# Attention's instructions in source order on every engine, the branch on one partition, masks built inside the branch

## The chip, the cores and the metric

One core of a Trainium2 chip runs the kernel. The metric is the device time of one execution in microseconds. Before the change the median of 3 runs was 667.44 us (664.49 to 668.09).

## What is computed

A windowed attention with sink keys, and two feed-forward layers behind it, in float32.

```python
scores = scale * np.matmul(q, k.transpose(0, 1, 3, 2))     # q, k, v: 2 x 8 heads x 768 x 64
keep = (pos[None, :] < n_sink) | ((rel >= 0) & (rel < window))   # n_sink 4, window 128
a = softmax(np.where(keep, scores, -1e9))
x = np.matmul(a, v)                                         # -> 1536 tokens x 512
h = x @ w_in                                                # 512 x 2048
g = np.where(h > 0, h, np.exp(np.minimum(h, 0)) - 1)
x = g @ w_out                                               # 2048 x 512
h = x @ w2_in
out = (np.maximum(h, 0) + alpha * np.minimum(h, 0)) @ w2_out
```

The weights come as float64, two 32-bit words each, and `n_sink` and `window` as 64-bit integers.

## The kernel before, in words

The program first loads the two limits (`ints`, L186), the first keys, queries, values and weights, works out from the limits whether the fast path may be taken (`flag_i`, L223), builds masks 0 and 1 (`make_mask_at`, L457) and branches (L721) into `fast_path` or `general_path`. Only the fast path runs here.

Queries are cut into blocks of 110 (seven per head), keys into the 128 to 256 columns that a block can see. Two heads lie in one 128-partition tile. A unit (`units`, L139) is one or two blocks of two heads; there are 32 units. Each unit goes through `scores` (TensorE score matmuls `qk`, L489; VectorE adds the mask and takes the extreme, L496; ScalarE takes the exponential with its sum, L501), `normalised` (two small VectorE operations, L511 and L514; GpSimd scales, L518), `transposed` (TensorE transposes `t`, L532; VectorE copies them to `pt`, L608) and `values` (TensorE value matmuls `x`, L553; ScalarE makes `xh`, L562, and VectorE the rest `xl`, L563). `matmul3` makes one product out of three with numbers split into a high and a low part (`xh`, `xl`, `wh`, `wl`, `gh`, `gl`).

The loop over steps s (L581) does, for each s, the scores of unit s, the values of unit s-2, one piece of fill, the normalisation of unit s and the transposes of unit s-1. Fill is round 0 of the first feed-forward layer for tokens whose attention is done: 32 pieces `g1` (`h`, L278 in `matmul3`) and `g2` (`o`) of 12 matmuls each over 220, 328 or 440 tokens. A step without fill gets a group of dummy matmuls (`keep_busy`, L238). `after` of a `g1` piece is ScalarE's L307 and L308, VectorE's `u` (L309), ScalarE's `gh` (L320) and GpSimd's `gl` (L321). In the first eight steps one half of round 0's weights is decoded in each (`decode_w`): two ScalarE instructions (L254, L255), four VectorE ones (L257, L260, L263, L266), ScalarE's `wh` (L269), and `wl` (L270) on VectorE for halves 0 to 3 and on GpSimd for 4 to 7. The raw weights have three buffers, the tiles `wx` and `wr` that a decode works in two.

Behind the loop `mlp_rounds` does the last token tile of round 0 and seven more rounds over three tiles of 512 tokens, each with eight more decodes for the round that follows.

A planner sets the order of the instructions on each engine's queue. It goes by the order of the source as priority, and by its own estimate of when an instruction can start: whatever can start goes first, so instructions of later code (of `mlp_rounds`, too) move ahead into gaps. Tiles are given out by the same planner.

Of the kernel before, what the change touches and what calls it, by code (L numbers as in the profile page):

```python
# [13 lines left out]
I32 = mybir.dt.int32  # L14
# [40 lines left out]
MS = {2: 1, 3: 2, 4: 5}  # L55
# [56 lines left out]
def attention_mlp2(  # L112
# [86 lines left out]
    for g in range(HP):  # L199
        if g:  # L200
            load_kq(g)
        if g < WPRE:
            o = HP * (2 * KTOT[0] + VCH[0] * 2 * D) + g * 2 * DM
            load_w(0, g, 0, room[:, o : o + 2 * DM].bitcast(I32).rearrange("p (n t) -> p n t", t=2))
        load_v(g)
    wfirst = dict(wraw)
    intf = const.tile([P, 2, 2], F32, tag="intf", name="intf")
# [9 lines left out]
    flag_f = const.tile([P, 2], F32, tag="flag_f", name="flag_f")  # L217
    flag_i = const.tile([P, 1], I32, tag="flag_i", name="flag_i")
    nc.vector.tensor_scalar(out=flag_f[:, 0:1], in0=win, scalar1=float(WIN), scalar2=None, op0=ALU.is_le)
    nc.vector.scalar_tensor_tensor(  # L220
        out=flag_f[:, 1:2], in0=win, scalar=1.0, in1=flag_f[:, 0:1], op0=ALU.is_ge, op1=ALU.mult
    )
    nc.vector.scalar_tensor_tensor(  # L223
        out=flag_i, in0=ns, scalar=float(SINK), in1=flag_f[:, 1:2], op0=ALU.is_le, op1=ALU.mult
    )
# [19 lines left out]
    def decode_w(pool, m, fc, io, sub=None):  # L245
# [35 lines left out]
    class Mlp:  # L281
# [7 lines left out]
        def g1(self, m, c0, n, fc):  # L289
# [12 lines left out]
            def after():  # L302
# [9 lines left out]
                else:  # L312
# [6 lines left out]
                    )  # L319
                nc.scalar.copy(gh, u)  # L320
# [5 lines left out]
        def g2(self, m, c0, n, r, d):  # L326
# [11 lines left out]
            def after():  # L338
# [4 lines left out]
                if r == NR - 1:  # L343
                    if m == 0:
                        xh, xl = (x[:, d, c0 : c0 + n] for x in xs)
                        nc.scalar.copy(xh, a)
                        nc.gpsimd.tensor_tensor(out=xl, in0=a, in1=xh, op=ALU.subtract)
                    else:
                        nc.sync.dma_start(out=out_t[d * P : d * P + P, c0 : c0 + n], in_=a)

            return after

    def run(pieces):

        pend = []
        for p, extra in pieces:
            if p is None:
                pend.pop(0)()
# [4 lines left out]
            if len(pend) > 1:  # L363
                pend.pop(0)()
        for a in pend:
            a()
# [6 lines left out]
    def mlp_rounds(mlp, items, wpools):  # L373
# [22 lines left out]
        def weights_step():  # L396
# [3 lines left out]
            for _ in decode_w(*order[j]):  # L400
                pass
# [25 lines left out]
    def make_mask(blk, rel, mk):  # L427

        for c, n, k in mask_runs(blk):
            k = 4 * S if k is None else k  # L430
            nc.gpsimd.iota(rel[:, c : c + n], pattern=[[-1, n]], base=Q0[blk] - k, channel_multiplier=1)
        nc.vector.tensor_scalar(
            out=mk, in0=rel.bitcast(U32), scalar1=win, scalar2=-NEG / SCALE, op0=ALU.is_ge, op1=ALU.mult
# [5 lines left out]
        masks[blk] = mk  # L439
# [12 lines left out]
    def make_mask_at(blk):  # L452
        o = sum(KW[i] for i in MASKS if i < blk)
        rel = tmp.tile([P, WMAX], I32, tag="rel", name=f"rel{blk}", bufs=1)
        make_mask(blk, rel[:, : KW[blk]], mask_t[:, o : o + KW[blk]])

    make_mask_at(0)  # L457
    make_mask_at(1)
# [4 lines left out]
    def fast_path():  # L463
# [10 lines left out]
        def scores(i):  # L474
# [6 lines left out]
            for blk in blks:  # L481
                n, (k0, w) = NQ[blk], SPAN[blk]
                for e in range(2):
# [7 lines left out]
                    )  # L491
            for j, blk in enumerate(blks):
# [12 lines left out]
            soft[i] = sb, st  # L505
# [33 lines left out]
        def values(i):  # L539
# [21 lines left out]
            def after():  # L561
                nc.scalar.copy(xh, px[:, :o])  # L562
# [215 lines left out]
```

## Time and profile before

| | before |
|---|---|
| median of 3 runs | 667.44 us |
| profiled execution | 667.86 us |
| its span, first to last instruction | 666.0 us |
| TensorE busy | 637.4 us, 96% |
| VectorE busy | 440.4 us, 66% |
| ScalarE busy | 313.9 us, 47% |
| GpSimd busy | 210.2 us, 32% |
| mean granted TensorE clock | 0.977 |

Busy time of TensorE is modelled, so a share of 96% does not say that it runs at its peak. In the rows PE is TensorE, PEld its weight loads, DVE VectorE, ACT ScalarE, POOL GpSimd, SP SyncE; L278 is line 278 of the kernel; PEclk is the granted clock as a share of 2.4 GHz, at full or at half. `out<-in` names the tiles.

### The profile page before, as it was taken

To read this page: it belongs to the slowest core of one execution; us is meant where nothing else is said; L and a number is where in the kernel's file an instruction comes from. 1 tells how busy PE (TensorE), PEld (TensorE's weight loads), DVE (VectorE), ACT (ScalarE), POOL (GpSimd) and SP (SyncE) were. 2 spreads that over 40 slices of the span, in tenths; PEclk is the share of its full clock that TensorE was granted. 3 is DMA by queue.
4 is the path that set the end of the run, shared out by engine and by line. 5 is a ranking of instruction groups with operands and counts; after the bars stand their busy time and mean duration, and the time that the engine had idled before them with its cause. 6 is when DMAs were issued, how large, how long until landed. Compare 5 with 4: busy or idle time off the path is not lost.

```text
span 666.0 us, 9595 instructions
## 1 busy us (share of the span) xinstructions
PE 637.4 (96%) x3412; PEld 524.9 (79%) x3412; DVE 440.4 (66%) x932; ACT 313.9 (47%) x710; POOL 210.2 (32%) x253
## 2 busy tenths in 40 slices
PE   6977999999989898999999999999999999999996
PEld 5646888888878676888888888888888888888885
DVE  5798566756399998576656786785569673443332
ACT  5576576747378775466546743543525220110010
POOL 3455344534122322232215364332123212331130
PEclk8796999999999999999999999999999999999999
DMA  7766325630034243031103120311212000000112
GB/s 225 209 169 186 105 66 134 156 101 2 1 126 158 95 135 118 2 126 63 64 21 107 63 64 5 122 64 63 65 63 64 32 0 1 0 2 0 64 50 83
DMA packets 21657, 52.87 MB, mean 79 GB/s; under 512 B 2656, under 2 KB 9824, under 8 KB 21600
## 3 DMA queue, kind: packets, MB, share of 16 engines
q1 hardware_dynamic: 21168, 52.05, 25.6%
q8 instruction: 29, 0.48, 0.3%
q14 instruction: 28, 0.23, 0.1%
q10 hardware_dynamic: 432, 0.12, 0.1%
HBM read 49.01 MB, written 3.15 MB: 78 GB/s over the span
## 4 chain that ended last, share of the span: by engine, by line
PE 78%; DVE 13%; ACT 3%; issue 2%; DMA 2%; POOL 1%; SPq 0%; ACTq 0%; DVEq 0%; POOLq 0%
PE o L278 36%; PE h L278 33%; PE x L553 4%; PE qk L489 3%; PE t L532 3%; DVE wx L263 3%; DVE wx L266 2%; DVE wx L257 2%; DVE wl L270 2%; DVE wx L260 1%; ACT s L501 1%; DVE pt L608 1%; DVE u L309 1%; DMA acc<-in_w_dram 1%; PE busy L238 1%
## 5 line engine op out<-in xcount | busy, mean ns | idle before, releaser
L321 POOL TENSOR_TENSOR gl<-u,gh 128x512 fp32r<-128x512 f32 (+3 forms) x104 | 131.9, 1268 | 339.0 <-ACT gh L320 330.5
L278 PE MATMUL o<-gh,wh 128*128 128x512 f32 (+3 forms) x416 | 157.4, 379 | 5.7 <-DVE u L309 5.7
L278 PE MATMUL h<-xh,wh 128*128 128x512 f32 (+3 forms) x416 | 158.2, 380 | 0.0
L278 PE MATMUL o<-gl,wh 128*128 128x512 f32 (+3 forms) x416 | 155.9, 375 | 1.0 <-POOL gl L321 0.9
L278 PE MATMUL h<-xl,wh 128*128 128x512 f32 (+3 forms) x416 | 156.5, 376 | 0.0
L278 PE MATMUL h<-xh,wl 128*128 128x512 f32 (+3 forms) x416 | 156.5, 376 | 0.0
L278 PE MATMUL o<-gh,wl 128*128 128x512 f32 (+3 forms) x416 | 155.3, 373 | 0.0
L320 ACT CAST gh<-u 128x512 fp32r<-128x512 f32 (+3 forms) x104 | 60.9, 586 | 135.8 <-DVE u L317 114.2
L342 DVE TENSOR_TENSOR acc<-o,acc 128x512 f32<-128x512 f32 x72 | 49.4, 688 | 75.1 <-PE o L278 74.7
L278 PEld LDWEIGHTS o<-gh,wh 128*128 128x128 f32 x416 | 78.0, 188 | 23.1 <-DVE u L309 8.0
L278 PEld LDWEIGHTS h<-xh,wh 128*128 128x128 f32 x416 | 79.2, 190 | 15.9 <-issue 0.3
L278 PEld LDWEIGHTS o<-gl,wh 128*128 128x128 f32 x416 | 78.2, 188 | 15.3 <-POOL gl L321 1.9
L278 PEld LDWEIGHTS h<-xh,wl 128*128 128x128 f32 x416 | 79.4, 191 | 13.6
L278 PEld LDWEIGHTS h<-xl,wh 128*128 128x128 f32 x416 | 79.4, 191 | 13.3
L278 PEld LDWEIGHTS o<-gh,wl 128*128 128x128 f32 x416 | 78.2, 188 | 13.5
L518 POOL TENSOR_SCALAR s<-s,st 110x250 f32<-110x250 f32 (+5 forms) x112 | 54.5, 504 | 74.6 <-DVE st L514 26.5
L269 ACT CAST wh<-wx 128x512 fp32r<-128x512 f32 x64 | 39.5, 619 | 69.6 <-DVE wx L266 32.0
L313 DVE TENSOR_SCALAR u<-h,alpha_sb 128x512 f32<-128x512 f32 x48 | 35.9, 748 | 46.6 <-PE h L278 46.6
L270 DVE TENSOR_TENSOR wl<-wx,wh 128x512 fp32r<-128x512 f32 x60 | 45.6, 763 | 23.9 <-ACT wh L269 22.1
L501 ACT ACTIVATE s<-s,st 110x250 f32<-110x250 f32 (+5 forms) x112 | 52.9, 474 | 14.8 <-DVE st L496 14.7
L266 DVE CUSTOM_DVE_ANT_0 wx<-wx,wq 128x1024 uint16<-128x1024 uint16 x64 | 58.0, 907 | 0.9
L263 DVE SCALAR_TENSOR_TENSOR wx<-wr,wx 128x512 int32<-128x512 int32 x62 | 55.3, 892 | 0.9
(53 smaller groups left out, 651.9 us busy)
## 6 DMA issues: line engine op xcount, KB each, us to landing
wr<-in_w_dram SPq DMA_DIRECT2D x62, 512.0 KB, 3.4
kq<-in_kq_dram SPq DMA_DIRECT2D x16, 237.0 KB, 4.0
vr<-in_vc_dram SPq DMA_DIRECT2D x8, 384.0 KB, 4.0
out_dram<-acc SPq DMA_DIRECT2D x12, 256.0 KB, 2.0
kq<-in_kq_dram SPq DMA_DIRECT2D x16, 180.0 KB, 3.7
vr<-in_vc_dram SPq DMA_DIRECT2D x8, 256.0 KB, 4.3
acc<-in_w_dram SPq DMA_DIRECT2D x2, 512.0 KB, 5.6
kq<-in_kq_dram SPq DMA_DIRECT2D x8, 110.0 KB, 2.7
```

The lines of the kernel that those rows point to most:

```text
L263: nc.vector.scalar_tensor_tensor(out=x, in0=high, scalar=-0x40000000, in1=x, op0=ALU.bitwise_and, op1=ALU.bitwise_or)
L266: nc.vector.tensor_tensor(out=x, in0=x, in1=r, op=ALU.add)
L269: nc.scalar.copy(wh, xf)
L270: (sub or nc.vector).tensor_tensor(out=wl, in0=xf, in1=wh, op=ALU.subtract)
L278: nc.tensor.matmul(out, a, c, start=(i == 0), stop=(i == n - 1))
L313: nc.vector.tensor_scalar(out=u, in0=hp, scalar1=0.0, scalar2=alpha_sb[:, fc : fc + 1], op0=ALU.min, op1=ALU.mult,)
L320: nc.scalar.copy(gh, u)
L321: nc.gpsimd.tensor_tensor(out=gl, in0=u, in1=gh, op=ALU.subtract)
L342: nc.vector.tensor_tensor(out=a, in0=po, in1=a, op=ALU.add)
L501: nc.scalar.activation(sb[:n, j, e, :w], sb[:n, j, e, :w], AF.Exp, bias=st[:n, 0, j, e : e + 1], scale=-1.0, accum_out=st[:n, 1, j, e : e ...
L518: nc.gpsimd.tensor_scalar(out=sb[:n, j, e, :w], in0=sb[:n, j, e, :w], scalar1=st[:n, 3, j, e : e + 1], scalar2=1.0, op0=ALU.mult, op1=ALU. ...
L553: nc.tensor.matmul(px[e * D : e * D + D, o : o + n], vr[:r, vs : vs + D], pt[:r, p0 : p0 + n], start=(k == 0), stop=(k == c - 1),)
```

## The change

The loop over attention's steps now stands inside a region in which every engine issues the region's instructions in the order in which the source writes them; where instructions from outside the region fall among them is still the planner's. The source of the loop is laid out for that: generators (`scores`, `values`, `decode_w`, the `after` functions) now yield between their parts, and the loop interleaves the parts. Within a step the order is: cast and subtraction of the weights decoded in the step before; `gh` and `gl` of the step before's fill; score matmuls, and reductions and exponentials of the unit's first block; value matmuls of unit s-2 and `xh`; the second block; `xl`; the four VectorE operations of this step's decode; the fill piece or dummies; the normalisation; transposes of unit s-1 and their copies; dummies once more where there was no fill; the first part of the fill's `after`; a second piece of fill if eight or more wait; the mask of the step; the two ScalarE instructions of the next decode; loads.

Besides: in steps up to 7 the second `pt` copy of a unit is ScalarE's instead of VectorE's. Fill starts one step earlier (`last_of` + 2). The branch flag is worked out on one partition from four words of its own small load (`int1`), ahead of the load of the limits on all partitions. The difference matrices of the masks (`distance`) are made on GpSimd before the branch, in tiles of their own; the masks themselves are made inside the branch, 0 and 1 ahead of the first step, 2, 3 and 4 behind steps 0, 1 and 5. Loads of the first keys and queries are split over two queues, and values are loaded later.

```diff
-MS = {2: 1, 3: 2, 4: 5}
+MS = {2: 0, 3: 1, 4: 5}
...
+    words = limits.bitcast(I32).rearrange("(o t) -> o t", o=1)
+    int1 = const.tile([1, 4], I32, tag="int1", name="int1")
+    nc.scalar.dma_start(out=int1, in_=words)
     ints = const.tile([P, 2, 2], I32, tag="ints", name="ints")
-    src = limits.bitcast(I32).rearrange("(o t) -> o t", o=1).to_broadcast([P, 4])
-    nc.scalar.dma_start(out=ints.rearrange("p a t -> p (a t)"), in_=src)
-    load_kq(0, queues=(nc.sync, nc.scalar))
+    nc.scalar.dma_start(out=ints.rearrange("p a t -> p (a t)"), in_=words.to_broadcast([P, 4]))
...
+    load_kq(0, queues=(nc.sync, nc.scalar))
+    load_kq(1, queues=(nc.sync, nc.scalar))
+    load_w_early(0)
+    load_kq(2)
+    load_w_early(1)
+    load_v(0)
+    load_kq(3)
+    load_v(1)
...
+    nc.vector.tensor_tensor(out=flag_f, in0=int1.bitcast(U32), in1=bound, op=ALU.is_lt)
+    nc.vector.tensor_reduce(out=flag_m, in_=flag_f, op=ALU.min, axis=mybir.AxisListType.X)
+    nc.vector.scalar_tensor_tensor(
+        out=flag_i, in0=int1[:, 2:3].bitcast(U32), scalar=0.5, in1=flag_m, op0=ALU.is_ge, op1=ALU.mult
+    )
...
         nc.vector.tensor_tensor(out=x, in0=x, in1=r, op=ALU.add)
+        yield
         wh = pool.tile([P, DM], F32R, tag=f"wh{io}", name=f"wh{nm}")
         wl = pool.tile([P, DM], F32R, tag=f"wl{io}", name=f"wl{nm}")
         nc.scalar.copy(wh, xf)
+        yield
         (sub or nc.vector).tensor_tensor(out=wl, in0=xf, in1=wh, op=ALU.subtract)
...
+            nc.scalar.copy(xh, px[:, :o])
+            yield
+            nc.vector.tensor_tensor(out=xl, in0=px[:, :o], in1=xh, op=ALU.subtract)
...
-            at_ = last_of[t * HP + HP - 1] + 3
+            at_ = last_of[t * HP + HP - 1] + 2
...
+        order = inner.enter_context(tc.manual_schedule())
+        make_mask(0)
+        make_mask(1)
         ws = halves(0)
-        load_w(*ws[WPRE])
+        for j in range(WPRE, WPRE + 3):
...
+            late = s - 1 in decodes
+            if late:
+                next(decodes[s - 1])
+            for a in gates:
+                done(a)
+            gates = []
+            if late:
+                done(decodes.pop(s - 1))
+            sc = scores(s) if s < nu else iter(())
+            next(sc, None)
+            vs = values(s - 2) if s >= 2 else iter(())
+            next(vs, None)
+            done(sc)
+            done(vs)
+            if s == 0:
+                decodes[0] = decode_w(wa, *ws[0], sub=nc.vector)
+                next(decodes[0])
+            if s in decodes:
+                next(decodes[s])
+            take = 1 if fill and fill[0][0] <= s else 0
+            after = fill.pop(0)[1]() if take else None
+            if not take and s < nu:
+                keep_busy(ps, "ps", BUSYN)
             if s < nu:
                 normalised(s)
-            copies = list(transposed(s - 1)) if 1 <= s <= nu else []
-            for a in afters:
-                a()
-            for out, in_ in copies:
-                nc.vector.tensor_copy(out, in_)
-            ready = len([f for f in fill if f[0] <= s])
-            if ready > FILL_MAX:
-                afters.clear()
-                fill_one()
-                for a in afters:
-                    a()
+            if 1 <= s <= nu:
+                for j, (out, in_) in enumerate(transposed(s - 1)):
+                    (nc.scalar.copy if j and s < len(ws) else nc.vector.tensor_copy)(out, in_)
+            if not take and s < nu:
+                keep_busy(ps, "ps", BUSYN)
+            if after:
+                after = after()
+                next(after)
+                gates.append(after)
+            if len([f for f in fill if f[0] <= s]) >= FILL_MAX:
+                after = fill.pop(0)[1]()()
+                next(after)
+                gates.append(after)
             for blk, at_ in MS.items():
                 if s == at_:
-                    make_mask_at(blk)
-            if s + WPRE + 1 < len(ws):
-                load_w(*ws[s + WPRE + 1])
+                    make_mask(blk)
+            if s + 1 < len(ws):
+                decodes[s + 1] = decode_w(wa, *ws[s + 1], sub=nc.vector if s + 1 < FG else nc.gpsimd)
+                next(decodes[s + 1])
+            if WPRE <= s and s + 3 < len(ws):
+                load_w(*ws[s + 3])
```

## Rows read from the trace of the kernel before

**Rows 1.** Busy time of the engines by stage (us from the span's start), clock and DMA.

```profile
core 0: us, PE busy (x) PEld busy (x) DVE busy (x) ACT busy (x) POOL busy (x), PEclk, DMA share, GB/s
7.50:66.40 58.90, 47.64 (x310) 35.16 (x310) 50.20 (x166) 39.58 (x117) 28.24 (x53) 0.77 0.71 205
66.40:179.70 113.30, 111.47 (x974) 94.01 (x974) 68.61 (x279) 66.91 (x232) 46.32 (x92) 1.00 0.31 83
179.70:258.00 78.30, 71.74 (x338) 58.95 (x337) 75.93 (x116) 59.60 (x111) 20.50 (x16) 1.00 0.37 121
258.00:660.60 402.60, 402.60 (x1777) 333.04 (x1775) 243.30 (x364) 146.34 (x248) 113.83 (x84) 1.00 0.16 51
```

**Rows 2.** Chain that ended last, shares of the span by engine.

```profile
PE 78%; DVE 13%; ACT 3%; issue 2%; DMA 2%; POOL 1%; SPq 0%; ACTq 0%; DVEq 0%; POOLq 0%
```

**Rows 3.** The same chain in order of time, 45 to 55 us: start, us, what.

```profile
45.39 1.84 DVE wx L257
...
48.69 1.70 POOL s L518 x3
...
51.09 1.24 POOL wl L270
...
52.35 0.68 ACT wx L254
53.04 1.93 ACT s L501 x8
```

**Rows 4.** Instructions in order of time, TensorE: start, us, operation, [idle <- releaser].

```profile
7.49 1.21 PE L489 MATMUL qk<-acc 64*110 64x110 f32 x8 [2.19 <-DVE mask L436]
...
46.09 1.09 PE L489 MATMUL qk<-kq 64*110 64x250 f32 x8
...
56.03 1.11 PE L489 MATMUL qk<-kq 64*110 64x256 f32 x8
...
66.37 0.66 PE L489 MATMUL qk<-kq 64*108 64x242 f32 x4
```

**Rows 5.** Groups by line and shape, 180 to 258 us: count, busy us, mean ns.

```profile
L266 DVE CUSTOM_DVE_ANT_0 wx<-wx,wq 128x1024 uint16<-128x1024 uint16 x18 | 17.2, 956 | 0.2
...
L257 DVE TENSOR_SCALAR wx<-wx 128x512 f32<-128x512 f32 x19 | 8.0, 419 | 0.4 <-ACT wx L254 0.2
...
L340 ACT COPY acc<-o 128x440 f32<-128x440 f32 x1 | 0.5, 527 | 1.9 <-PE o L278 1.9
```

**Rows 6.** The same of 60 to 165 us.

```profile
L501 ACT ACTIVATE s<-s,st 110x250 f32<-110x250 f32 x24 | 11.8, 493 | 0.8 <-DVE st L496 0.8
...
L496 DVE CUSTOM_DVE_ANT_0 s<-qk,mask 110x250 f32<-110x250 f32 x24 | 9.0, 414 | 0.0
...
L608 DVE COPY pt<-t 125x440 f32<-125x440 f32 x13 | 7.9, 610 | 1.7 <-PE t L532 1.5
...
L514 DVE RECIPROCAL st<-st 110x4 f32<-110x4 f32 x16 | 2.8, 177 | 0.5
...
L511 DVE TENSOR_SCALAR st<-st 110x4 f32<-110x4 f32 x16 | 2.7, 170 | 16.8 <-ACT s L501 16.7
...
L309 DVE SCALAR_TENSOR_TENSOR u<-u,h 128x220 f32<-128x220 f32 x7 | 2.6, 374 | 0.0
```

**Rows 7.** The same of 10 to 60 us.

```profile
L257 DVE TENSOR_SCALAR wx<-wx 128x512 f32<-128x512 f32 x10 | 7.2, 717 | 0.6 <-ACT wx L254 0.6
...
L254 ACT ACTIVATE wx<-wr 128x512 f32<-128x512 f32 x8 | 5.4, 672 | 4.9 <-POOL wl L270 4.1 <-DMA wr<-in_w_dram 0.7
...
L270 POOL TENSOR_TENSOR wl<-wx,wh 128x512 fp32r<-128x512 f32 x4 | 5.1, 1264 | 0.0
```

**Rows 8.** Chain in order of time: a fill piece at half clock, and at full.

```profile
62.49 2.83 PE h L278 x12
...
86.06 1.53 PE h L278 x12
```

More of the change, by code (lines that the diff above doesn't have):

```diff
@@ L197, in load_w, with load_w_early @@
         wraw[m, fc, io] = raw
[L199 to L205, printed above, removed]
-    wfirst = dict(wraw)
+    def load_w_early(g):
+        o = HP * (2 * KTOT[0] + VCH[0] * 2 * D) + g * 2 * DM
+        load_w(0, g, 0, room[:, o : o + 2 * DM].bitcast(I32).rearrange("p (n t) -> p n t", t=2))
+    load_kq(0, queues=(nc.sync, nc.scalar))
[6 more added lines that the diff above has]
+    load_v(1)
+    wfirst = dict(wraw)
+    bound = const.tile([1, 4], F32, tag="bound", name="bound")
+    for i, most in enumerate((SINK, 0, WIN, 0)):
+        nc.gpsimd.memset(bound[:, i : i + 1], most + 0.5)
+    flag_f = const.tile([1, 4], F32, tag="flag_f", name="flag_f")
+    flag_m = const.tile([1, 1], F32, tag="flag_m", name="flag_m")
+    flag_i = const.tile([1, 1], I32, tag="flag_i", name="flag_i")
+    nc.vector.tensor_tensor(out=flag_f, in0=int1.bitcast(U32), in1=bound, op=ALU.is_lt)
[3 more added lines that the diff above has]
+    )
     intf = const.tile([P, 2, 2], F32, tag="intf", name="intf")
@@ L349, in after, with done @@
                         nc.sync.dma_start(out=out_t[d * P : d * P + P, c0 : c0 + n], in_=a)
+                yield
             return after
+    def done(steps):
+        for _ in steps:
+            pass
     def run(pieces):
@@ L399, in weights_step @@
                 load_w(*order[j + 2][1:])
-            for _ in decode_w(*order[j]):
-                pass
+            done(decode_w(*order[j]))
             state["at"] = j + 1
@@ L431, in make_mask @@
             nc.gpsimd.iota(rel[:, c : c + n], pattern=[[-1, n]], base=Q0[blk] - k, channel_multiplier=1)
+        return rel
+    def make_mask(blk):
+        o = sum(KW[i] for i in MASKS if i < blk)
+        masks[blk] = mk = mask_t[:, o : o + KW[blk]]
         nc.vector.tensor_scalar(
-            out=mk, in0=rel.bitcast(U32), scalar1=win, scalar2=-NEG / SCALE, op0=ALU.is_ge, op1=ALU.mult
+            out=mk, in0=rels[blk].bitcast(U32), scalar1=win, scalar2=-NEG / SCALE,
+            op0=ALU.is_ge, op1=ALU.mult,
         )
@@ L450, in attention_mlp2 @@
     mask_t = const.tile([P, sum(KW[i] for i in MASKS)], F32, tag="mask", name="mask")
[L452 to L458, printed above, removed]
+    relp = ctx.enter_context(tc.tile_pool(name="relp", bufs=1))
+    rels = {blk: distance(blk) for blk in MASKS}
     alpha_sb = const.tile([P, NFC], F32, tag="alpha", name="alpha_sb")
@@ L559, in values @@
             xh, xl = (x[:, hp, c0 : c0 + o] for x in xs)
[L561 to L565 removed]
+            nc.scalar.copy(xh, px[:, :o])
+            yield
+            nc.vector.tensor_tensor(out=xl, in0=px[:, :o], in1=xh, op=ALU.subtract)
         nu = len(units)
@@ L580, in fast_path @@
             load_v(g, at)
+        decodes = {}
+        gates = []
         for s in range(nu + 2):
-            afters = []
-            def fill_one():
-                if fill and fill[0][0] <= s:
-                    afters.append(fill.pop(0)[1]())
-                elif s < nu:
-                    keep_busy(ps, "ps", BUSYN)
-            if s < len(ws):
-                decode = decode_w(wa, *ws[s], sub=nc.vector if s < FG else nc.gpsimd)
-                next(decode)
-            if s < nu:
-                scores(s)
@@ L627, in fast_path @@
                     load_v(g + LB, at)
+        for a in gates:
+            done(a)
         while fill:
-            fill.pop(0)[1]()()
+            done(fill.pop(0)[1]()())
         inner.close()
```

38 lines of the change are left out of this document (12 added, 26 removed).

## The prediction, made before the changed kernel was run

> **What bounds the kernel now.** The time by stage comes first [rows 1]. The 666.0 us span has four stages. From 258.0 to 660.6 us TensorE is busy without a gap; these are the feed-forward rounds, whose code the change leaves alone. From 179.7 to 258.0 us VectorE is busy 75.9 of 78.3 us, because it decodes the weights of rounds 1 and 2 beside the last tile of round 0. From 66.4 to 179.7 us TensorE has 111.5 of 113.3 us, VectorE 68.6: attention and the fill (round 0's matmuls put between attention's steps) share TensorE, and TensorE is the bound. From 7.5 to 66.4 us VectorE has 50.2 of 58.9 us, TensorE 47.6 with a mean clock of 0.77, ScalarE 39.6, GpSimd 28.2. In these nine first steps VectorE decodes eight halves of weights and does the softmax of units 0 to 8. So the chain that ends the kernel is 78% TensorE and 13% VectorE [rows 2], and what a new order in attention can win lies in the first 66 us, or is lost again in the 113 us behind them.
>
> Next, the chain inside the worst stretch [rows 3]. The score matmuls of step 7 start at 46.09, of step 8 at 56.03, of step 9 at 66.37 [rows 4]: two steps of ten microseconds, where the first seven took (46.09 - 7.49)/7 = 5.5 each. The chain is there no single busy engine. It goes from a VectorE decode operation held for 1.84 us (its mean in the rounds is 0.42 [rows 5]) to the scaling on GpSimd, to GpSimd's weight subtraction, to the next decode's first ScalarE instruction, which had waited for that subtraction, and only behind it come the exponentials of the unit that everybody needs. One instruction of a later decode, queued ahead of the softmax, stops ScalarE and so VectorE and TensorE.
>
> **Part by part.** I number the terms and sum them against the profiled execution's 667.86 us, which is 1.9 us more than its span and 0.4 us above the median 667.44.
>
> 1. Second `pt` copy to ScalarE in steps 1 to 7. Seven copies of 440 columns leave VectorE at 0.61 us each [rows 6]: 7 x 0.61 = 4.3 us out of the stage that VectorE bounds. ScalarE takes them at 0.53 us for 440 columns [rows 5]: 39.6 + 7 x 0.53 = 43.3 us, still under VectorE's 50.2 - 4.3 = 45.9. Covered, though not by much: -4.3 us.
>
> 2. The order. VectorE stands idle 58.9 - 50.2 = 8.7 us in the stage, and I also count in the part of its busy time that is only held time: ten L257 at 0.72 against 0.42, 3.0 us [rows 5, 7]. From below, all 8.7 us could go, since the new order queues a decode's ScalarE pair at the end of a step, its four VectorE operations behind the next step's scores, its cast and subtraction a step later: each has a step's time to become ready. That removes the wait of [rows 3]. From above, the order brings waits of its own. In step 0 VectorE reaches the decode behind the four score reductions, but ScalarE does four exponentials and then the pair, so VectorE waits about 4 x 0.49 + 0.67 - 3 x 0.41 = 1.4 us [rows 6, 7]; before, other units' reductions were put there. Every step VectorE's normalisation waits for the last exponential, and the `pt` copies, the `u` operation and the next step's reductions are queued behind it. And from step 5 on GpSimd does the weight subtraction (1.26 us [rows 7]) just before VectorE's decode. Between -8.7 and +9 I take 0: the long wait gone, the same amount back in small ones. It is nearest to the first seven steps, where the planner's order already ran 5.5 us a step and VectorE was nearly full.
>
> A held VectorE operation is what [rows 3] show at 45.39 us, and the Trainium skill (SBUF — State Buffer, Who interferes with whom) says why: of a VectorE instruction in its two-port mode and a GpSimd one, the second waits until the first ends. This trace agrees, 1.84 against 0.42 us. By that rule the new order would hold L257 once in each of the steps 5 to 7, 3 x (1.84 - 0.42) = 4.3 us where the old one held 3.0, and the sum would be 664.3.
>
> 3. Weights of round 1. The planner has already put two decodes of round 1 into this stage (there are ten L257 up to 60 us, round 0 needs eight [rows 7]). The change pins only the order inside attention, so it may do that again. If it does, nothing changes; if not, VectorE saves two decodes here and does them after 180 us, where it is the bound again: L257 and L266 alone are 0.42 + 0.96 there [rows 5], at least 2.8 us for two, at most twice that with the two other operations between. I take the former: 0.
>
> 4. Fill. It starts at step last+2 instead of last+3, and a second piece is taken at 8 waiting ones instead of 9. One piece of 12 matmuls moves into the nine early steps, where TensorE has room: 1.53 us at full clock [rows 8]: -1.5 us. Against it the last steps lose their cover: before, two pieces ran beside the last units and one after them; now the last unit's value matmuls wait for the `pt` copy (0.61 [rows 6]) and hand-overs with nothing between: +0.9 us. A piece also waits for the last unit's `xh` and `xl` of the same step, but only its last quarter reads them, so that is hidden behind nine matmuls.
>
> 5. Fillers. Steps without fill get two groups of dummy matmuls instead of one. TensorE is no bound there, if its clock stays up; at the low clock a piece of 12 took 2.83 instead of 1.53 us [rows 8]. Bounds -1 (clock kept up) to +3 (the filler is what is ahead of the transposes). I take 0.
>
> 6. Start. The branch looks at one partition's four words, and masks 0 and 1 move behind the branch. The first score matmul waited until 7.49 us for masks [rows 4]; the masks still need the limits on all partitions and are still ahead of the first reductions on VectorE's queue. The difference matrices for all five masks are made before the branch on GpSimd, which is idle then. 0, bounds -1 to +1.
>
> 7. In 66.4 to 179.7 us the order in the source (scores, values, fill, transposes) is the one that TensorE's rows already have. 0, bounds in the rivals.
>
> Sum: -4.3 + 0 + 0 - 1.5 + 0.9 + 0 + 0 = -4.9; 667.86 - 4.9 = **663.0 us**. Step 9's scores should then start at about 62 us, and attention end at about 175 instead of 179.7.
>
> **Rivals.** (a) The waits go and little comes back: term 2 at -6 instead of 0, 657 us. For it: the chain of [rows 3] is a queueing accident that this order cannot have. Against: only two steps of nine had it.
>
> (b) Slower: the fixed order becomes a loop through VectorE and ScalarE that is longer than TensorE's step. One turn is the first reduction 0.41, four exponentials 4 x 0.49, the two small operations 0.35, two `pt` copies 1.22 and `u` 0.37 [rows 6]: 4.3 us and half a dozen hand-overs, while TensorE's step is 113.3/25 = 4.5 us [rows 1]. The source also puts the `xh` cast between the exponentials and the `gh` cast ahead of them. It decides from the point where hand-overs and casts exceed 0.2 us a step. At 0.4 us in 24 steps it is +9.6: 672.6 us. For it: the margin is small. Against: the old order has nearly the same loop and TensorE lost only 1.8 us in the stage; VectorE's `xl` leaves the loop.
>
> (c) No difference, 667: the copies moved to ScalarE make ScalarE late, since from step 5 on it has the exponentials, pair, cast, copy and the fill's operations, and VectorE waits for it at the normalisation; or the two decodes of term 3 go behind 180 us and take back 2.8 to 5.6.
>
> (d) The change doesn't do what it says: instructions from outside the region still fall where the planner puts them, and a decode of round 1 queued ahead of an exponential repeats the wait of [rows 3]; about 3 us of the 4.9 are lost, 666. It goes with (c).
>
> **Chances.** Forecast 0.42, (a) 0.18, (c) and (d) 0.24, (b) 0.16. What a measurement of this kernel can tell from no change is about 0.5%, 3.3 us. Of the forecast's 0.42 some 0.32 lie more than that below 667.4, with all of (a) and a little of (c): faster 0.54; same 0.30; slower 0.16. The range takes in (a) with 2 us more and the lower half of (b): 655 to 671.
>
> **What would show it.** Step 9's score matmuls at 62 us; no ScalarE wait for the weight subtraction over 1 us before 66 us; 440-column copies on ScalarE; attention's end near 175; the stage to the gapless part still some 78 us. If step 9 is early and attention's end is not, (b) holds, and TensorE's waits for the `pt` copies in 66 to 180 us will say so. If step 9 is at 66 or later, term 1 or 5 failed: look at who VectorE waits for, and at TensorE's clock. If step 9 is at 57, (a). Wrong altogether it would be if the stage from 179.7 on moved by more than the two decodes.

## The result and the profile after

The changed kernel takes 672.1 us (median of 10 runs, 670.5 to 673.6) where the kernel before took 668.2 beside it. The ratio is 1.007, 95% interval 1.0051 to 1.009: slower by 0.7%, and outside the range of 655 to 671.

The stage windows of the changed kernel, in the columns of [rows 1], cut at its own ends of the stages:

```profile
7.50:66.40 58.90, 42.81 (x348) 35.38 (x346) 49.39 (x153) 42.16 (x125) 25.86 (x43) 0.87 0.68 198
66.40:179.40 113.00, 111.17 (x956) 94.24 (x956) 68.15 (x276) 66.28 (x231) 44.96 (x89) 0.98 0.31 85
179.40:256.90 77.50, 73.30 (x339) 59.02 (x338) 75.03 (x116) 59.20 (x111) 20.79 (x16) 1.00 0.37 122
256.90:665.80 408.90, 408.86 (x1776) 333.00 (x1775) 244.88 (x366) 146.95 (x249) 113.43 (x84) 1.00 0.15 50
```

Two things are to be seen. Attention ends at 179.4 us, the old 179.7: what it won is gone by then. And the gapless rounds take 408.9 us with the same 1776 or 1777 matmuls that took 402.6 [rows 1], at the same full clock, with no idle time. Their code is the part that the change left alone. The gapless part starts 1.1 us earlier than before and is 6.3 us longer: together 5.2 us, the growth of the span from 666.0 to 671.1 us but for 0.1.

In the chain of waits each group of 48 matmuls is one row (start, us, what). Before, every one took the same:

```profile
258.06 10.88 PE h L278 x48
268.94 10.88 PE o L278 x48
```

After, two durations are mixed:

```profile
278.71 10.91 PE h L292 x48
289.62 11.20 PE o L292 x48
300.82 10.92 PE h L292 x48
311.74 11.20 PE o L292 x48
322.94 11.19 PE h L292 x48
```

Step 9 of attention begins when it was forecast. TensorE's score matmuls in order of time, steps 0, 7, 8, 9 and 10, to be read against [rows 4] (before, step 10 began at about 70.6):

```profile
6.26 0.82 PE L510 MATMUL qk<-acc 64*110 64x110 f32 x8
...
45.68 1.66 PE L510 MATMUL qk<-kq 64*110 64x250 f32 x8 [0.40 <-DVE st L518]
...
55.35 1.11 PE L510 MATMUL qk<-kq 64*110 64x256 f32 x8
...
61.21 0.66 PE L510 MATMUL qk<-kq 64*108 64x242 f32 x4
...
73.18 1.11 PE L510 MATMUL qk<-kq 64*110 64x256 f32 x8
```

Step 9 starts 5.2 us earlier, at 61.2 where about 62 was forecast. Then it lasts 12.0 us. Steps 7, 8 and 9 took 9.9, 10.3 and 4.2 us before and take 9.7, 5.9 and 12.0 now, so one long step has moved on by one and the other has stayed. The chain in step 9:

```profile
55.32 3.86 DMA wr<-in_w_dram
...
59.27 0.68 ACT wq L267
...
60.53 0.69 ACT s L523 x3
...
61.44 0.98 ACT s L523 x4
62.42 0.56 ACT wx L266
...
64.09 0.85 DVE wx L275
...
64.96 0.85 DVE wx L278
65.81 0.54 DVE pt L638
...
66.39 1.79 PE x L575 x16
68.18 2.83 PE o L292 x12
```

A load of raw weights lands at 59.2; a ScalarE instruction (L267) of round 1's weights that had waited for it stands ahead of step 8's exponentials (L523). It belongs to the third decode of round 1: there are four L267 between 54 and 67 us, but of L266, the other half of a decode's ScalarE pair, there are two (53.8 and 62.3 us) and the next comes at 181.3. The last of each are

```profile
62.32 0.65 ACT L266 ACTIVATE wx<-wr 128x512 f32<-128x512 f32 x1
...
65.84 0.66 ACT L267 ACTIVATE wq<-wr 128x512 int32<-128x512 uint32 x1 [2.64 <-DVE wx L278]
```

The four VectorE operations in the chain (L269 to L278) belong to the second decode. They stand ahead of the copy to `pt` (L638), for which TensorE's value matmuls wait 4.5 us. After that wait the fill piece of 12 takes 2.83 us, the half-clock price of [rows 8]; the granted clock from 61.2 to 73.2 us is 0.72 in the mean.

### The profile page after: what moved, and what is told of

Its sections match the earlier page's. It is cut to its first block, busy times and chain, and to the rows that moved or that the text cites. A ratio compares the mean times of both kernels' runs of the same rounds, so it can differ in the third digit from the quotient of the medians.

```text
span 671.1 us, 9665 instructions
## 1 busy us (share of the span) xinstructions
PE 642.0 (96%) x3444; PEld 527.0 (79%) x3444; DVE 440.8 (66%) x925; ACT 316.5 (47%) x717; POOL 207.9 (31%) x257
## 4 chain that ended last, share of the span: by engine, by line
PE 80%; DVE 11%; ACT 4%; issue 3%; POOL 1%; DMA 1%; ACTq 0%; DVEq 0%; POOLq 0%; SPq 0%
PE o L292 37%; PE h L292 34%; PE x L575 3%; PE t L554 2%; PE qk L510 2%; DVE wx L275 2%; ACT s L523 2%; DVE wl L284 1%; DVE wx L269 1%; DVE wx L278 1%; PE busy L250 1%; DVE u L323 1%; DVE pt L638 1%; DVE wx L272 1%; ACT wx L266 1%
## 5 line engine op out<-in xcount | busy, mean ns | idle before, releaser
L292 PE MATMUL o<-gh,wh 128*128 128x512 f32 (+3 forms) x416 | 159.2, 383 | 3.7 <-DVE u L323 2.0
L540 POOL TENSOR_SCALAR s<-s,st 110x250 f32<-110x250 f32 (+5 forms) x112 | 52.7, 488 | 86.0 <-DVE st L536 42.6
L523 ACT ACTIVATE s<-s,st 110x250 f32<-110x250 f32 (+5 forms) x112 | 53.1, 476 | 20.8 <-DVE st L518 20.8
L278 DVE CUSTOM_DVE_ANT_0 wx<-wx,wq 128x1024 uint16<-128x1024 uint16 x64 | 58.0, 906 | 1.3
L267 ACT ACTIVATE wq<-wr 128x512 int32<-128x512 uint32 x62 | 41.5, 669 | 32.9 <-DVE wx L278 29.4
```

The costliest lines, as they stand in the source:

```text
L267: nc.scalar.activation(r, low.bitcast(U32), AF.Copy, scale=2.0**-29)
L292: nc.tensor.matmul(out, a, c, start=(i == 0), stop=(i == n - 1))
L523: nc.scalar.activation(sb[:n, j, e, :w], sb[:n, j, e, :w], AF.Exp, bias=st[:n, 0, j, e : e + 1], scale=-1.0, accum_out=st[:n, 1, j, e : e ...
L540: nc.gpsimd.tensor_scalar(out=sb[:n, j, e, :w], in0=sb[:n, j, e, :w], scalar1=st[:n, 3, j, e : e + 1], scalar2=1.0, op0=ALU.mult, op1=ALU. ...
```

## The experiments

"Attention end" is the start of the first matmul of round 0's last tile, and the stage behind it runs to the first of the gapless 48-groups. Step 9 to 10 is the time between their score matmuls. The kernel before was timed beside each set of runs: 668.2 us beside the changed kernel, 667.6 beside e1 to e4, 667.2 beside e5 to e8, 667.4 beside e9 to e12, 668.0 beside e13 and e14. Medians of different sets can differ by up to 0.9 us for that alone; the ratios take it out.

| kernel | median us | ratio to before, interval | step 9 to 10 | attention end | gapless from |
|---|---|---|---|---|---|
| changed kernel | 672.1 | 1.007, 1.0051 to 1.009 | 12.0 | 179.4 | 256.9 |
| e5 aligned | 666.17 | 0.9977, 0.9962 to 0.9992 | 12.9 | 179.5 | 257.05 |
| e6 no hoist tried | 661.4 | 0.9925, 0.9909 to 0.9941 | 11.1 | 174.0 | 251.5 |
| e7 two decodes by hand | 658.64 | 0.9877, 0.9859 to 0.9894 | 5.8 | 171.4 | 248.85 |
| e8 aligned, planner's order | 660.86 | 0.9911, 0.9895 to 0.9928 | 5.3 | 172.8 | 250.3 |
| e9 late loads | 659.4 | 0.9872, 0.9854 to 0.9889 | 5.6 | 173.3 | 250.65 |
| e10 copies back | 659.22 | 0.9873, 0.9859 to 0.9888 | 5.5 | 172.4 | 249.8 |
| e11 e7, planner's order | 662.4 | 0.9917, 0.9901 to 0.9933 | 5.2 | 175.0 | 252.5 |
| e12 old fill | 660.73 | 0.9898, 0.9883 to 0.9913 | 4.4 | 171.3 | 249.7 |
| e13 none in attention | 659.96 | 0.9887, 0.9861 to 0.9913 | 5.6 | 169.7 | see there |
| e14 decodes by hand, early | 660.81 | 0.9898, 0.9874 to 0.9921 | 9.8 | 176.25 | 253.1 |

The columns on the right come from one profiled execution each. How far such times can be trusted, equal programs show: e3 and e4 below have the instructions of the kernel before in the same order, e1, e2 and e5 those of the changed kernel. The first score matmul starts at 7.5, 5.6 and 5.8 us in the former, at 6.3, 5.8, 5.8 and 6.3 in the latter; step 9 at 66.4 to 66.8 and at 60.1 to 61.2; attention ends at 179.7 to 180.1 and at 178.0 to 179.5. So the early step 9 is clear of chance, and a difference of a microsecond or so between two profiles is not.

### Why the rounds grew

The change makes five difference tiles of its own, 4384 bytes in a partition. They lie between the first weight tiles (`wa`) and the second (`wb`) with the hidden activations (`gb`), and 4384 is not a multiple of 512. Before, all of these and the `x` tiles stood at the same remainder modulo 512; after, the odd rounds' weights and the hidden activations are 288 bytes further on. The groups of 11.2 us are `o` with even-round weights and `h` with odd-round ones: those whose weights and moving operand come from different sides.

**e1**: the changed kernel, one difference tile 32 bytes wider. **e2**: everything moved by 32 bytes together. **e3**: the kernel before, its one difference scratch 32 bytes wider. **e4**: the kernel before with each weight tile of the odd rounds 32 bytes longer, so that many distances occur (of its edit the lines for `wh` are shown; those for `wl` are alike).

```diff
 e1
-        rel = relp.tile([P, KW[blk]], I32, tag=f"rel{blk}", name=f"rel{blk}")
+        pad = 8 if blk == 0 else 0
+        rel = relp.tile([P, KW[blk] + pad], I32, tag=f"rel{blk}", name=f"rel{blk}")[:, : KW[blk]]
 e2
-    alpha_sb = const.tile([P, NFC], F32, tag="alpha", name="alpha_sb")
+    alpha_sb = const.tile([P, NFC + 8], F32, tag="alpha", name="alpha_sb")[:, :NFC]
 e3
-        rel = tmp.tile([P, WMAX], I32, tag="rel", name=f"rel{blk}", bufs=1)
+        rel = tmp.tile([P, WMAX + 8], I32, tag="rel", name=f"rel{blk}", bufs=1)
 e4
+        pad = 8 if pool is not wa else 0
-        wh = pool.tile([P, DM], F32R, tag=f"wh{io}", name=f"wh{nm}")
+        wh = pool.tile([P, DM + pad], F32R, tag=f"wh{io}", name=f"wh{nm}")[:, :DM]
...
```

> The changed kernel with one difference tile 32 bytes wider, so that the tiles behind it (weights of odd rounds, gh and gl) move by 32 bytes and stand, modulo 64, where the feature tiles and the weights of even rounds stand. Address theory: in the gapless rounds every 48 matmuls take 10.88 us as before the change, none 11.20; 19 of 37 groups lose 0.3 us each, so the profiled execution is some 6 us under the changed kernel's 673, at 666 to 668, ratio to the kernel before 0.995 to 1.0. Order theory (the rounds are slower because of what the fixed order does to queues or loads): still a mix of 10.9 and 11.2, ratio 1.007.

> The changed kernel with the last constant tile 32 bytes wider, so that all tiles behind it move together: the features and even weights now start on a multiple of 64, odd weights and gh, gl 32 off. Theory that stationary and moving operand must agree modulo 64: nothing changes, the same groups of 48 at 11.20 us, about 672. Theory that a tile must by itself start on a multiple of 64: other groups are slow. Theory that any added pad repairs it: 10.88 everywhere.

> The kernel before with a scratch tile 32 bytes wider, which lies between the weights of even and odd rounds; instructions and order are meant to stay as they are. Address theory: groups of 48 with features against odd weights, and gh, gl against even weights, go from 10.88 to 11.20 us; half of 36 groups, so 6 us slower, ratio 1.008 to 1.010. Order theory: no difference, ratio 1.000.

> The kernel before with each of the sixteen weight tiles of odd rounds 32 bytes wider, so that their starts step through 32-byte offsets against the features and gh, gl: 0, 32, 64, 96 and on to 480. One look at the matmul spacing by offset. If the period is 64: 226.7 ns at offsets 0, 64, 128 and 233.3 at 32, 96, 160. If it is 128 or more, some of 64, 192 are slow too. Order theory: 226.7 everywhere.

e1 gave 670.71 us, ratio 1.0053 (1.0033 to 1.0073): a part came back, not all. In its chain the even-weight `o` groups fell to 11.01, the odd-weight `h` groups stayed:

```profile
310.15 11.01 PE o L292 x48
321.16 11.19 PE h L292 x48
```

So the addresses matter, and 64 bytes, the period that I had assumed, is wrong. e2 gave 672.5 us in a single run with the same groups: moving all of it together by 32 bytes changes nothing, so what counts is the distance. e3 is the cleanest proof. The kernel before, with no instruction added, dropped or moved, loses in the rounds what the change lost there: 673.91 us, ratio 1.010 (1.0072 to 1.0127), and its window of the gapless part and two of its groups read

```profile
258.00:667.00 409.00, 409.00 (x1777) 333.08 (x1775) 243.39 (x364) 146.50 (x248) 113.93 (x84) 1.00 0.16 50
```

```profile
312.98 11.20 PE o L278 x48
324.18 11.19 PE h L278 x48
```

The distance is the weights' address less the moving operand's, modulo 512 bytes; the number is the mean time from one matmul's start to the next, worked out from the trace's start times and the tiles' addresses. Where whole groups share a distance, the reading is direct: 226.7 ns at 0 in the kernel before; 233.3 at 224 and at 288 in the changed kernel; 230.6 at 192 and 233.3 at 320 in e1; 233.3 at 32 and at 480 in e3. That is why e1 won a part back in the `o` groups alone.

e4 (673.15 us, a single run) has more distances, but mixed: of three matmuls in a row two use a `wh` tile and the third the `wl` tile, whose distance is 128 bytes more. Only the time from the first to the second lies between two matmuls of one distance:

```
distance of the two        0     32     64     96    256    288    320    352
distance of the third    128    160    192    224    384    416    448    480
first to second, ns    227.4  233.4  232.3  232.3  231.5  232.3  235.4  233.8
mean of the three, ns  231.3  233.0  232.0  231.6  232.2  230.4  232.7  231.5
```

Of the distances of the two only 0 gives 227 ns, and where all three have distance 0 the mean is 226.8 to 227.0. No single number can be given for a distance that occurs only in the third place: 416 would read 224.7 ns when the time is counted to the earlier of two matmuls, and 234.3 when it is counted to the later.

**e5** tests the period of 512: the same tile 224 bytes wider, so that all distances are 0 again.

```diff
+        pad = 56 if blk == 0 else 0
+        rel = relp.tile([P, KW[blk] + pad], I32, tag=f"rel{blk}", name=f"rel{blk}")[:, : KW[blk]]
```

> The changed kernel with one difference tile made 224 bytes wider, so that the weight tiles wb and the hidden activations stand at the same remainder modulo 512 bytes as the x tiles and wa; nothing else differs. Address theory, period 512: every group of 48 matmuls in the rounds goes back to 10.88 us, the loss of 6.3 us in the gapless part goes, 672.1 - 6.3 = 665.8 us; attention runs as in the changed kernel (end near 179.4, gapless part from near 256.9). Rival (the spacing hangs on something that the order of the code behind attention brings, queues or neighbours on other engines): groups of 11.2 us stay, 670 to 672 us.

666.17 us, 5.9 less than the changed kernel (6.2 by the two ratios), with no instruction added, dropped or moved. The gapless part is back at 402.7 us and every group at 10.88:

```profile
257.00:659.70 402.70, 402.61 (x1777) 333.22 (x1775) 244.89 (x366) 146.91 (x249) 113.24 (x84) 1.00 0.16 51
```

```profile
311.45 10.88 PE o L292 x48
322.33 10.88 PE h L292 x48
```

What in the hardware makes the distance matter, no run here shows.

### Where attention lost its gain

All that follow contain e5's padding. **e6** gives the decodes' work tiles out anew behind attention, which should have kept round 1's decodes out of it. **e7** writes two of these decodes into the loop at steps 10 to 19, one VectorE operation in a step. **e14** writes the same two at steps 7 to 9, near where the planner had put them, with the four VectorE operations of each in one step. **e9** and **e13** begin none in the loop; their loads are issued at step 32, in e9 on SyncE, in e13 on ScalarE.

```diff
 e6
...
+        wdec["pool"] = inner.enter_context(tc.tile_pool(name="wdec", bufs=2))
...
+        wdec["pool"] = outer.enter_context(tc.tile_pool(name="wdec_r", bufs=2))
 e7
...
+            for i, h in enumerate(halves(1)[:2]):
+                if h in begun and 11 + 5 * i <= s < 15 + 5 * i:
+                    next(begun[h])
...
+            for i, h in enumerate(halves(1)[:2]):
+                if s == 8 + i:
+                    load_w(*h)
+                if s == 10 + 5 * i:
+                    begun[h] = decode_w(lambda: wbs[0], *h, fine=True)
+                    next(begun[h])
 e14, against e7
+                if h in begun and s == 8 + i:
+                    for _ in range(4):
+                        next(begun[h])
...
+                if s == 5 + i:
+                    load_w(*h)
+                if s == 7 + i:
 e13 (e9 without the queue)
+                if s == nu:
+                    load_w(*h, queue=nc.scalar)
```

> As e5_align512, and the work tiles of the decodes belong to attention and are given out anew behind it, so that no decode of round 1 can be queued inside attention. Theory (rival (d) of the prediction: two decodes of round 1 ahead of the exponentials at step 9 cost the early gain): score matmuls of step 10 follow those of step 9 by about 5 to 6 us instead of 12, attention ends near 175 us instead of 179.4; the two decodes come back behind attention, where VectorE is the bound, and take 3 to 6 us there, so the total is 664 to 667 us. Rival (the low TensorE clock at 61 to 73 us or the fill itself makes step 9 long): step 10 stays near 73 us, attention ends near 179, and the total is 668 to 671 us.

> As e5_align512, and two decodes of round 1 are written into the loop by hand: loads in steps 8 and 9, the two ScalarE instructions at the end of steps 10 and 15, one of the four VectorE operations in each of the steps 11 to 14 and 16 to 19, the cast and the subtraction in the rounds. Theory (it is the place of the two decodes that costs, not their work): attention ends near 175 to 176 us and the stage to the gapless part stays at 77 to 78 us, total about 661 us. Rival (VectorE's and ScalarE's loop is full in those steps, so that any decode there costs its own time): attention ends at 179 or later, total 665 us or more.

> As e7_late2, but the first two decodes of round 1 are not begun in attention at all: their loads are issued in step 32 of 34, so they can run only behind it. It prices what the prediction's term 3 bounded at 2.8 to 5.6 us (two decodes back in the stage that VectorE bounds). Theory: attention ends as in e7_late2 or up to 1 us earlier (171 to 172 us), the stage to the gapless part grows from 77.3 to 80 to 83 us, total 661 to 664 us. Rival (that stage has slack, so decodes ahead of it buy nothing): the stage stays under 78.5 us and the total is at or below 659 us.

> As e9_behind, with the two loads issued from ScalarE's queue at the end of step 32, so that no decode of round 1 can run before attention's last two steps. Theory (term 3: VectorE bounds the stage behind attention, so two decodes more there cost 2.8 to 5.6 us): attention ends near 171 us, the stage to the gapless part takes 80 to 83 us, total 660 to 663 us. Rival (VectorE works ahead in that stage on decodes that nobody needs yet, so two more only shift later ones): the stage stays within 1 us of 77.3, total 657.5 to 659 us.

> As e7_late2 with the same two decodes written at the end of steps 7 and 8 (ScalarE pair) and in one go in steps 8 and 9 (the four VectorE operations), where the planner had put them in the changed kernel. Theory (the place costs): step 9 to step 10 takes 8 to 12 us instead of 5.8, attention ends at 176 to 180 instead of 171.8, total 663 to 667 us. Rival (the loss came from queueing that the planner chose, ahead of the exponentials, and not from the steps): attention ends within 1.5 us of 171.8, total 658 to 660.5 us.

e6 did not do what it was made for: the trace still has two decodes of round 1 on VectorE at 57.4 and 59.3 us, now behind step 8's exponentials. It is faster than expected (661.4), by an earlier step 8, but step 9 to 10 still takes 11.1 us. It tells nothing of a kernel without these decodes.

e7 gave 658.64 us, better than both kernels and 2 us better than expected. Steps 9 and 10, and the windows of step 9 and of the stage behind attention:

```profile
58.65 0.66 PE L519 MATMUL qk<-kq 64*108 64x242 f32 x4
64.45 1.11 PE L519 MATMUL qk<-kq 64*110 64x256 f32 x8
```

```profile
58.70:64.50 5.80, 5.41 (x55) 4.64 (x54) 4.06 (x14) 2.61 (x10) 3.38 (x7) 1.00 1.02 322
64.50:171.50 107.00, 104.47 (x910) 87.90 (x909) 68.21 (x273) 66.73 (x228) 43.41 (x86) 1.00 0.34 89
171.50:248.90 77.40, 72.46 (x337) 58.95 (x338) 75.03 (x116) 59.22 (x111) 20.80 (x16) 1.00 0.38 123
```

Step 9 takes 5.8 us at full clock, where e5 has 12.9 us at a mean of 0.74; attention ends 8.1 us earlier, and the stage behind it still takes 77.4: the two decodes cost nothing visible in the stage behind it. The L267 of the third and fourth decode, which the planner still places, come at 90.3 and 106.1 us, behind the two written pairs, so e7 moves all four. The kernel before had the same two decodes in its steps 7 and 8 (their L257 are at 53.1 and 59.7 us), so what e7 wins by their place need not be something that the change had lost; the kernel before with its decodes placed in this way was not tried. The fill piece of step 9 has the full-clock duration:

```profile
59.14 0.51 DVE pt L651
...
59.69 1.13 PE x L584 x16
60.83 1.53 PE o L299 x12
```

Step 7 keeps its length even here: 10.2 us at a mean clock of 0.67. VectorE's operations on the last half of round 0's weights (45.8 to 48.0 us) stand ahead of the `pt` copy, in the order of the source itself, TensorE's value matmuls wait 3.1 us, and the piece behind them takes 2.83 us. It is the pattern of step 9, and no run was made to remove it.

e14 stands between the two expectations: 660.81 us, 2.2 above e7 by the medians and 1.4 by the ratios, whose intervals overlap; 0.3 above the rival's range, 2.2 below the theory's. Its profile is of its slowest execution (663.03 us), so the profile shows the mechanism and not its usual price. Step 9 takes 9.8 us there. Its chain:

```profile
61.38 0.70 DVE wx L279
...
62.10 0.69 DVE wx L284
...
63.09 0.51 DVE pt L652
...
63.65 1.37 PE x L584 x16
65.01 2.83 PE o L299 x12
```

The decode's four VectorE operations come ahead of the `pt` copy, TensorE waits 2.8 us, and the next piece runs at half clock. In the profiles the place, four operations in one step included, costs 9.8 - 5.8 = 4.0 us of the 12.9 - 5.8 = 7.1. The other 3.1 came with the planner's placing. The traces of e14 and of the changed kernel show where it begins: step 8's score matmuls start at 55.37 and 55.35 us, but VectorE's first reduction of them (first row: e14, second: changed kernel) 1.9 us apart, since in the changed kernel the first decode's VectorE operations run from 55.2 to 58.7 among the work of step 8.

```profile
57.02 0.42 DVE L527 CUSTOM_DVE_ANT_0 s<-qk,mask 110x256 f32<-110x256 f32 x1
...
58.88 0.41 DVE L518 CUSTOM_DVE_ANT_0 s<-qk,mask 110x256 f32<-110x256 f32 x1
```

The first exponential follows 1.5 us later in e14 and 1.2 in the changed kernel, so the ScalarE instruction that waits 0.76 us for its load adds nothing that this comparison shows. No run took one of the two away by itself.

e9 missed its aim too. SyncE, with little in its queue, issued the loads early, and the two decodes ran at 149.3 and 153.2 us, inside attention, so its stage of 77.3 us behind attention says nothing of term 3. e13 has none there: VectorE's first round-1 decode starts at 172.4 us. Attention ends earliest of all, at 169.7, and the debt shows later, where TensorE waits for a decode of the next weights at 260 us:

```profile
254.78 4.54 DMA wr<-in_w_dram
...
259.42 0.67 ACT wq L267
260.09 0.53 ACT u L329
...
261.45 11.19 PE o L299 x48
272.64 10.88 PE h L299 x48
```

From attention's end to the `h` group that is the third of the gapless ones in e7 it takes 272.64 - 169.71 = 102.9 us, in e7 (248.85 + 2 x 10.88) - 171.41 = 99.2. (The 11.19 of this `o` group, the first behind a wait, is no effect of addresses: from its first start to the next group's it is 11.03, and the groups after it but the last take 10.88.) Two decodes moved behind attention therefore cost 3.7 us there; the 1.7 us that come back in attention are hardly more than equal programs differ by. The total, 659.96, is 1.3 above e7 with intervals that overlap.

### What the other terms are worth

**e8** is e5 and **e11** is e7 without the region that pins the order; **e10** is e7 with the second `pt` copy back on VectorE; **e12** is e7 with the fill as before.

```diff
 e8, e11
-        order = inner.enter_context(tc.manual_schedule())
 e10
-                    (nc.scalar.copy if j and s < len(ws) else nc.vector.tensor_copy)(out, in_)
+                    nc.vector.tensor_copy(out, in_)
 e12
-            at_ = last_of[t * HP + HP - 1] + 2
+            at_ = last_of[t * HP + HP - 1] + 3
-            if len([f for f in fill if f[0] <= s]) >= FILL_MAX:
+            if len([f for f in fill if f[0] <= s]) > FILL_MAX:
```

> As e5_align512 without the line that pins the order inside attention: the planner orders the same source. Theory (the pinned order is what brings the early gain of some 5 us at step 9): step 9's score matmuls fall back to about 65 us, as before the change (66.4), and the total is 667 to 670 us. Rival (the gain at step 9 comes from the copies on ScalarE and the parts that the source now spreads, whoever orders them): step 9 stays near 61 us and the total is within 2 us of e5_align512.

> As e7_late2 without the line that pins the order. It tells what the pinned order itself is worth once the decodes of round 1 are not what differs. Theory (the pinned order is a loss or nothing as such: in e8_noman, where the planner ordered, step 9 was only 0.8 us later than in e5_align512 and the total 5.3 us shorter): total 657 to 661 us, within 2 us of e7_late2. Rival (the pinned order wins some 4 to 5 us in the first 60 us): step 9 at 63 us or later and total 662 to 665 us.

> As e7_late2 with the second pt copy of steps 1 to 7 back on VectorE. It prices term 1 of the prediction (4.3 us). Theory (VectorE bounds the first steps, so each copy costs its time there): step 9's score matmuls at about 63 us instead of 59.1, attention ends some 4 us later, total 662 to 663 us. Rival (ScalarE is as full as VectorE in those steps and has the exponentials on the same path): step 9 within 1 us of 59.1, total 658 to 660 us.

> As e7_late2 with the fill's start and its limit as before the change (three steps behind a tile's last unit, a second piece from nine waiting). It prices term 4 of the prediction (-1.5 us for a piece moved into the early steps, +0.9 for the tail, together -0.6). Theory: total 658.5 to 660 us, first fill about one step later. Rival (the piece lands in steps where the TensorE clock is low or VectorE and ScalarE are full, so starting earlier costs): total 656 to 658 us, with earlier score matmuls in steps 5 to 9.

Step 9's score matmuls start at 60.8 us in e8, 63.0 in e11 and 57.6 in e12. In e10 the row is

```profile
59.88 0.66 PE L519 MATMUL qk<-kq 64*108 64x242 f32 x4
```

e8 was expected at 667 to 670 and gave 660.86, 5.3 below e5: with the same source the planner's own order beats the pinned one (4.4 by the ratios). It places round 1's decodes at 45 to 55 us, with the loop's instructions in view instead of around a fixed list; that this is why it wins is argued. Its steps 6 and 7 take 9.8 and 10.3 us, as steps 7 and 8 did before. e11 shows the other side: with the two decodes written by hand, pinned is 3.8 us better than planned (658.64 against 662.4; 2.7 by the ratios). Without the pin the planner moved them up again (ScalarE's second instruction of the pair at 45.9 and 47.0 us), so e11 prices the pin and the place that it holds together. e10 is 0.6 us above e7 by the median and 0.3 below it by the ratios, with intervals that overlap, and its step 9 is 1.2 us later, as much as equal programs differ by. The rival stands: where 4.3 us were at stake, no loss clear of noise is seen. e12 is 2.1 us above e7 by the median and 1.4 by the ratios, with intervals that overlap, and 0.8 in the profiles. Attention ends at the same time (171.3 against 171.4), and the stage behind it is 0.9 us longer, as in the kernel before (78.3).

## Why the prediction was wrong, point by point

**What it left out.** The step that failed is the first one: "the feed-forward rounds, whose code the change leaves alone", which the sum then held at 402.6 us. Unchanged code is not an unchanged stage. The change adds tiles, tiles move addresses, and 18 groups at 11.20 instead of 10.88 (5.8 us) and 0.02 or 0.03 us on each of the others (0.5) make the 6.3 us. e3 and e5 show it in both directions. The diff had it in sight ("in tiles of their own"), but the trace of before gave no hint, as every group there is alike. The text did name this place as the one that would make it wrong altogether.

**Term 3, the decodes of round 1.** "If it does, nothing changes: 0" is the second failure. The planner did put two decodes ahead again, one step later than before, at steps 8 and 9, and there their place costs 7.5 us (e5 against e7, 666.17 to 658.64; 6.7 by the ratios). They stood in long steps before, too (9.9 and 10.3 us), so how much of the 7.5 is new with the change no run tells. Rival (d) named the instructions and their cause. Its 666 us is what the aligned e5 gave, 666.17, but that is luck, as the sum of two errors: the place costs more than its 3 us, and the rest of the change with the decodes placed is better than the forecast. It saw the wait on ScalarE alone; the traces show VectorE's part standing ahead of the reductions and of the `pt` copy, and TensorE's wait followed by the half clock, which makes the piece behind it 1.3 us longer. The other half of the term holds: moved behind attention, two decodes cost 3.7 us there, inside 2.8 to 5.6.

**Term 1, the copies: -4.3.** The copies went to ScalarE at the price that was worked out; seven of 440 columns appear in two groups of the changed kernel between 10 and 60 us:

```profile
L638 ACT COPY pt<-t 110x440 f32<-110x440 f32 x4 | 2.0, 510 | 1.8 <-PE t L554 1.8
...
L638 ACT COPY pt<-t 122x440 f32<-122x440 f32 x3 | 1.6, 517 | 0.8 <-PE t L554 0.8
```

But in e10 taking them off VectorE shows no gain clear of noise, where 4.3 us would show. The stage was read as bounded by VectorE from its busy share (50.2 of 58.9); that busy time taken away there turns into waiting is argued.

**Term 2, the order: 0.** "That removes the wait of [rows 3]" rests on a misreading. Of the ten L254 up to 60 us eight start before 52.3, so the one at 52.35 in [rows 3] is the first of round 1, which stands outside the region; the pin can't reach it, and (a)'s "queueing accident that this order cannot have" falls with it. The term's value lay between the bounds, and its sign hangs on the decodes: the pin costs 5.3 us when the planner places them around it, and is worth up to 3.8 when they are written down. The rule of the Trainium skill (SBUF — State Buffer, Who interferes with whom) agreed in kind: L269 was held for 1.26 us at 37.9 and 1.13 us at 52.9 beside a GpSimd subtraction, 0.42 otherwise. That is 1.5 us, in two steps of three, where I had worked out 4.3.

**Terms 4 and 6.** The fill was forecast at -1.5 + 0.9. In e12 its sign is the forecast one; only the 0.9 us of the stage behind attention stand out from the differences between equal programs. The first score matmul starts at 6.26 us where [rows 4] have 7.49, but with the instructions of the kernel before it starts at 5.59 in e3 and at 5.84 in e4, so no gain at the start is shown.

**Rivals.** (b) did not happen, though its 672.6 us is the nearest to what was measured: from step 10 on, e7 has 107.0 us for what TensorE fills with 104.5, at full clock. (a)'s size, -6 for the waits, is seen only in e7, which stands 8.5 us (1.2%) under the kernel before, 3.6 better than the forecast; but there it took two decodes written down by hand, which the change doesn't do.

So -4.9 was forecast. Without the addresses the change as it was made gives 666.17 - 667.18 = -1.0 (-1.5 by the ratio); with the decodes placed as well it gives 658.64 - 667.18 = -8.5. From there the decodes' place puts on 7.5 and the addresses 5.9, which makes +4.9, the changed kernel's 672.1 against the same 667.18; by the ratios it is -8.2 + 6.7 + 6.2 = +4.7.

## What to carry to other kernels

When a change adds, drops or resizes a tile, compare the addresses of the large operands before and after, and, for matmuls like these, keep weights and moving operands at the same remainder modulo 512 bytes; a stage with unchanged code can move by 1.5%. When a region's order is pinned, the code outside it must be told where to stand as well: list what the planner used to slip in, and write it in or keep it out. A busy share of 85% on an engine does not make its instructions worth their duration; take one away on the chip before you count it.

## What the hardware showed that was not expected

The time from one matmul of 128 x 512 to the next, weights and moving operand both in SBUF, depends on the distance of the two addresses: 226.7 to 227.4 ns at a multiple of 512 bytes and 230.6 to 235.4 ns at ten other distances between 32 and 480, with a full granted clock in both cases (1.00 in the windows). A common shift of 32 bytes changes nothing (e2). No idle time shows in the busy rows, so only the durations of equal groups give it away.
